# Gated mix of attention with a memory and a gated feed-forward layer: matmuls of ones and whole loads at the start, transposes in halves, rows split at the head of a step

## The chip, the cores and the metric

One NeuronCore of a Trainium2 chip runs the whole program. The metric is the device time of one execution in microseconds (us), the median of several runs. The five engines of the core run side by side and are told apart as in the profile: PE (matmul, with PEld for its weight loads), DVE (vector), ACT (scalar), POOL (general) and SP, whose queue issues nearly all DMAs.

## The reference

The input x has 2048 rows of 576 numbers. Two branches are computed from it and mixed row by row:

```python
x = A_x
g = _sigmoid((x * gate_w).sum(-1, keepdims=True))
a = _A_ref(x, A_wq, A_wk, A_wv, A_wo, A_beta)   # attention with a memory
b = _B_ref(x, B_w_gate, B_w_up, B_w_down)       # (gelu(x@w_gate) * (x@w_up)) @ w_down
return g * a + (1 - g) * b
```

Branch A has 32 heads of 18 numbers and cuts the 2048 rows into 4 segments of 512. In each segment it computes causal softmax attention within the segment, and beside it a read of a memory M that the earlier segments have written (`phi(q) @ M` over `phi(q) @ z`); the two are mixed by a gate for each head, and the result is multiplied by wo. Branch B has a hidden layer of 4608. All in float32.

## The kernel before, in words

To keep float32 accuracy on f16 matmuls, each operand is scaled by a power of two and split into a high and a low f16 word; a product is three matmuls (high by high, high by low, low by high). High words are made by ACT (a copy with a scale), low words by DVE or POOL (a subtraction). The scales come from sums of squares over the whole weight, so each weight is first summed (`square_sum`, `sum_squares`, L80), then scaled.

**The start** (L596 to L669). SP loads x of segment 0 in three pieces (`load_x16`, L123) and the values' weights wv in pieces of rows and of column halves (`load_v`, L415: half `b`, group `g` of `VG`), one half-piece behind each piece of x, then the weights of q and k (`load_qk`). While the scales aren't known, the values of segment 0 are computed in float32 from the raw x and wv (`first_words`, L512): four row blocks for the first column half in four PSUM banks, then four for the second half (banks `vb`). `scale_x` (L136), `scale_v` (L433) and `scale_sum(0, ...)` (L97, for q and k) each add up their sums with a matmul of ones (L85, or L140) and end in six to seven short DVE instructions. `low_x` (L157) makes the low words of x, `put_rows` (L480) takes the value rows out of PSUM, its second part `rest` being queued in `later` and run by `finish_later`. `make_qk` makes the two words of one tile of q and k weights (L103 on ACT, L104 on DVE), which `project` (L453) then multiplies with x.

**The segments** (L772 to L821). For segment s the value rows are `vrows(s, q, b)` (L505, banks `dn`, of which there are two, L312 to L315), with `key_rows`, `recall` and `memorize` for the memory between them (bank `U` and `pv`); then nine projections.

**The main loop** (`step`, L1078). 72 steps, each with one hidden tile f of 128 (two steps a tile) for a pair of segments c and e, and one pair of attention problems (2k and 2k + 1). Products of a pair of segments share matmuls in Strassen's manner (`product`, `rest`, L1012 to L1024) in the banks V, G (X) and U (Y). For each attention problem a: `score_piece` (L871) computes the scores on PE and takes their maximum on DVE (L887); `powers` (L892) is the exponential on ACT (L897, L900); `pair_rows(a, 0)` and `(a, 1)` (L902) make high words on ACT (L909) and low words on POOL (L910); `turn_rows` (L911) transposes both words by one DMA of 20 blocks of 128 by 128 (L915); `values` (L917) multiplies them with the values on PE (L929); `normalize` takes the result out on DVE. The hidden rows: `gelu` on ACT, `hidden` (L997) on DVE, `hidden_pair` (L999) splits them into words on ACT (L1001) and POOL (L1002), for c within the step, for e by way of `late_hidden` in the next one. They are in tiles `gl`, of which there are two. `weights_first`, `weights_high`, `weights_low` prepare weights for later steps: POOL's scaling is `scale_g` (L250) and `scale_d` (L287). `down` (L967, L975) is the last product of branch B and runs in pieces between the others.

The order on PE, ACT, DVE and POOL is the order in the program (a manual schedule of these four); SP's queue isn't written out by hand: a scheduler places each DMA, and each waits for its buffers and for the DMA eight before it.

**The end** (`finish`, L1200). In steps 67 to 71 the rows of wo are loaded, summed, scaled (`pair_of`, L102, over pieces of rows in the last three of these steps), then come the output products.

Of the kernel before, what the change touches and what calls it, by code (L numbers as in the profile page):

```python
# [10 lines left out]
F16 = mybir.dt.float16  # L11
# [7 lines left out]
P = 128  # L19
# [22 lines left out]
def kernel(ctx: ExitStack, tc: tile.TileContext, xs, wqk, wv, wo, wgu, wd, beta, out):  # L42
# [80 lines left out]
    def load_x16(c, then=None):  # L123
        x_raw[c] = []
        x_sq[c] = flat(wts.tile([P, 2, 16 * P], F16, name="pairg", tag="pairg", bufs=2)).bitcast(BF16)
        for i, (k0, n) in enumerate(XG):
            r = raw_tile()
            sp.dma_start(r[:, : n * L], flat(xs[c, :, k0 : k0 + n]))
            x_raw[c].append(r)
            if then:  # L130
                then(i)
# [264 lines left out]
    with tc.tile_pool(name="prj", bufs=2, side="right", reuse_waits="tile") as pp:  # L396
# [18 lines left out]
        def load_v(b, g):  # L415
            ks = slice(VG[g][0], VG[g][-1] + 1)
            sp.dma_start(raw_v[:, ks, VB[b]], wv[:, ks, VB[b]])

        def square_sum(o, r, on_act):
            if on_act:  # L420
                junk = pa.tile([P, D], F32, name="krow", bufs=2).bitcast(BF16)
                act.activation(junk[:, : r.shape[1]], r, AF.Square, accum_out=o)
            else:
                sum_squares(o, r)

        def stat_v(b):
            for k in range(KT):
                square_sum(wst[:, KT * b + k : KT * b + k + 1], raw_v[:, k, VB[b]], b == 1)

        def stat_qk(j):  # L430
            square_sum(wst[:, 10 + j : 11 + j], raw_qk[:, j], j % 2 or j == 8)

        def scale_v():  # L433
            scale_sum(1, wst[:, 0 : 2 * KT])

            dve.tensor_scalar(usc, wsc[:, 1:2], xsc[:, 0:1], 2.0**-14, OP.mult, OP.mult)
# [159 lines left out]
        with tc.manual_schedule(engines=ORDERED):  # L596
            pool.memset(ones, 1.0)
            pool.memset(onesb, 1.0)
            load_x16(0, lambda g: load_v(0, g))
            for g in range(3):  # L600
                load_v(1, g)
# [5 lines left out]
            stat_v(0)  # L607
# [4 lines left out]
            stat_v(1)  # L612
# [55 lines left out]
            dve.tensor_scalar(gh[:, 1], gh[:, 0], -1.0, 1.0, OP.mult, OP.add)  # L668
            outscale(0, 1)  # L669
# [161 lines left out]
    with tc.tile_pool(name="keep", bufs=2, side="right", reuse_waits="tile") as kp, ExitStack() as tail:  # L831
# [70 lines left out]
        def pair_rows(a, i):  # L902

            p = prob[a]
            if i == 0:
                pairs16[a] = ap_.tile([P, 2, 10 * P], F16, name="ph", bufs=2)
            h = pairs16[a]
            cols = (slice(6 * P, 10 * P), slice(0, 6 * P))[i]
            act.activation(h[:, 0, cols], p[:, cols], AF.Copy)  # L909
            pool.tensor_tensor(h[:, 1, cols], p[:, cols], h[:, 0, cols], OP.subtract)  # L910

        def turn_rows(a):
            prob.pop(a)
            turned_p[a] = ap_.tile([P, 20, P], F16, name="pt", bufs=2)
            sp.dma_start(turned_p[a], pairs16.pop(a).rearrange("p a b -> p (a b)"), transpose=True)  # L915
# [162 lines left out]
        def step(v):  # L1078
# [12 lines left out]
            done = (k - 5) // 4 if i4 == 3 and 0 <= (k - 5) // 4 < H // 2 else None  # L1091
            weights_first(fb, i4)
# [5 lines left out]
            if late_hidden:  # L1098
                hidden_pair(*late_hidden.pop())
# [13 lines left out]
            V = ahead.pop(v) if v in ahead else first_product(v)  # L1113
# [28 lines left out]
            if v == 0:  # L1142
                scales_out(1)
                scale_g(2)
# [55 lines left out]
        def finish(i):  # L1200
# [87 lines left out]
```

## Time and profile before

| | us |
|---|---|
| median of 3 runs | 1651.63 (1650.98 to 1653.91) |
| the profiled execution | 1651.15 |
| its span in the profile | 1649.4 |
| PE busy | 1624.4 |
| DVE, POOL, ACT busy | 1268.4, 1162.2, 1085.9 |
| DMA transposes of probabilities | 128 issues, median 3.13 each |

The span runs from the first to the last instruction; 1.75 us of the profiled execution lie around it. In the rows of the timeline the first two numbers are the start and the duration in us, then the engine, the line of the kernel, the operation, the tile written and those read, and in square brackets how long the engine had been idle before it and what ended that.

### The profile page before, as it was taken

What the parts mean: (1) busy time and instruction counts of PE and PEld (TensorE: products, weight loads), DVE (VectorE), ACT (ScalarE), POOL (GpSimd) and SP (SyncE); (2) the same over time, 40 slices, a digit from 0 to 9 for tenths busy, and PEclk for the clock granted to TensorE, in tenths of its full rate; (3) what the DMA queues carried; (4) which work ended last, traced back from release to release, by engine and by line L of the source; (5) the groups of instructions that cost most, each with busy time, mean ns of one, the idle gap of its engine ahead of it and who ended that gap; (6) DMA issues with size and microseconds to landing.
All of it is one profiled execution on the core that took longest, in us unless ns stands there. A gap on an engine that the chain in (4) does not pass through costs nothing.

```text
span 1649.4 us, 31958 instructions
## 1 busy us (share of the span) xinstructions
PE 1624.4 (98%) x11884; PEld 982.7 (60%) x11884; DVE 1268.4 (77%) x3138; ACT 1085.9 (66%) x1786; POOL 1162.2 (70%) x1057
## 2 busy tenths in 40 slices
PE   8999998999999999999999999999999999999999
PEld 4656753655566555666555565555566555565577
DVE  5666785888788888878887878788788888776643
ACT  6665446777777777776777677777777777763200
POOL 2232657788888889787979788788879798885300
PEclk9999999999999999999999999999999999999999
DMA  6632443565656575666656575757566565635451
GB/s 213 215 112 88 147 136 68 119 133 106 131 110 128 112 128 113 129 114 129 133 109 126 108 142 103 139 103 130 119 140 123 120 130 103 133 72 122 87 124 64
DMA packets 462348, 200.54 MB, mean 122 GB/s; under 512 B 421232, under 2 KB 431728, under 8 KB 461680
## 3 DMA queue, kind: packets, MB, share of 16 engines
q1 hardware_dynamic: 462192, 198.50, 55.2%
q8 instruction: 93, 1.52, 0.4%
q14 instruction: 63, 0.52, 0.1%
HBM read 82.60 MB, written 27.26 MB: 67 GB/s over the span
## 4 chain that ended last, share of the span: by engine, by line
PE 82%; DVE 5%; DMA 5%; ACT 4%; POOL 2%; issue 2%; SPq 0%; DVEq 0%; ACTq 0%
PE dn L975 21%; PE U L1017 14%; PE V L1017 10%; PE G L1017 10%; DMA pt<-ph 4%; PE st L881 3%; PE pv L929 3%; PE V L1024 3%; PE st L312 3%; PE dn L312 2%; PE st L302 2%; PE U L1024 2%; PE G L1024 2%; PE G L302 1%; ACT pf L900 1%
## 5 line engine op out<-in xcount | busy, mean ns | idle before, releaser
L975 PE MATMUL dn<-paird,hh 128*128 128x288 f16 x3402 | 486.3, 286 | 0.0
L1017 PEld LDWEIGHTS <-pairg 128*128 128x128 f16 x3024 | 289.9, 98 | 276.4 <-issue 4.3
L910 POOL TENSOR_TENSOR ph<-pf,ph 128x512 f16<-128x512 f32 (+1 forms) x256 | 371.3, 1450 | 84.1 <-ACT ph L909 52.3
L975 PEld LDWEIGHTS <-hh 128*128 128x128 f16 x3456 | 336.7, 97 | 137.7
L983 DVE SCALAR_TENSOR_TENSOR acc<-dn,ev,acc 128x288 f32<-128x288 f32 x535 | 268.2, 512 | 69.8 <-PE dn L975 66.7
L900 ACT ACTIVATE pf<-pf,mb,esc 128x512 f32<-128x512 f32 (+3 forms) x512 | 293.0, 642 | 2.9
L1002 POOL TENSOR_TENSOR hh<-gl,hh 128x512 f16<-128x512 f32 x144 | 188.6, 1310 | 140.1 <-ACT hh L1001 140.1
L887 DVE CUSTOM_DVE_ANT_0 pf<-st,mask 128x512 f32<-128x512 f32 (+3 forms) x512 | 228.8, 483 | 73.9 <-PE st L881 73.8
L1017 PE MATMUL U<-xt,pairg 128*128 128x512 f16 x864 | 210.0, 379 | 0.6 <-DVE gl L1136 0.6
L1017 PE MATMUL G<-x,pairg 128*128 128x512 f16 x864 | 210.0, 379 | 0.0
L909 ACT ACTIVATE ph<-pf 128x512 f16<-128x512 f32 (+1 forms) x256 | 184.3, 720 | 0.0
L283 POOL TENSOR_TENSOR pairg<-raw,pairg 128x512 f16<-128x512 f32 (+2 forms) x144 | 168.5, 1190 | 8.3 <-ACT pairg L279 8.3
L1007 ACT ACTIVATE gl<-gl,sc 128x512 f32<-128x512 f32 x144 | 103.4, 719 | 82.8 <-DVE gl L1151 41.2
L897 ACT ACTIVATE mb<-mx,esc 128x4 f32<-128x4 f32 x128 | 37.2, 290 | 183.4 <-DVE mx L887 183.3
L1001 ACT ACTIVATE hh<-gl 128x512 f16<-128x512 f32 x144 | 89.6, 622 | 81.4 <-DVE gl L997 81.4
L250 POOL TENSOR_SCALAR raw<-raw,sc 128x640 f32<-128x640 f32 x72 | 137.0, 1915 | 0.0
L881 PE MATMUL st<-kt,qt 72*128 72x512 f16 (+3 forms) x512 | 111.7, 299 | 1.6 <-DVE mx L887 1.6
L1017 PE MATMUL V<-x,pairg 128*128 128x512 f16 x432 | 105.0, 379 | 2.2 <-DVE gl L1116 2.1
L1017 PE MATMUL U<-x,pairg 128*128 128x512 f16 x432 | 104.8, 378 | 0.3 <-DVE gl L1151 0.3
L1017 PE MATMUL V<-xt,pairg 128*128 128x512 f16 x432 | 105.0, 379 | 0.0
L1007 ACT ACT_TABLE_LOAD x66 | 84.7, 1283 | 24.6 <-DVE gl L1137 23.9
L1024 PEld LDWEIGHTS <-pairg 128*128 128x128 f16 x576 | 56.3, 98 | 68.1
(252 smaller groups left out, 2527.6 us busy)
## 6 DMA issues: line engine op xcount, KB each, us to landing
raw<-in_wgu_dram SPq DMA_DIRECT2D x36, 640.0 KB
rawd<-in_wd_dram SPq DMA_DIRECT2D x36, 288.0 KB
qk<-stage SPq DMA_DIRECT2D x36, 256.0 KB
qt<-qk SPq DMA_DIRECT2D x128, 72.0 KB
kt<-qk SPq DMA_DIRECT2D x128, 72.0 KB
vp<-vstage SPq DMA_DIRECT2D x16, 296.0 KB
vt<-vp SPq DMA_DIRECT2D x16, 296.0 KB
orow<-oa SPq DMA_DIRECT2D x16, 288.0 KB
```

The costliest lines, as they stand in the source:

```text
L283: pool.tensor_tensor(spot(f, *p, 1), raw_g[f][:, p[0] : p[1]], spot(f, *p, 0), OP.subtract)
L881: pe.matmul(o[:, off : off + n], q[:, e * L + qi * P : e * L + (qi + 1) * P], kt[:, e * L : e * L + n], start=True, stop=True)
L887: dve.tensor_tensor_reduce(prob[a][:, COL[qi] : COL[qi + 1]], o[:, off : off + n], mask[:, L - n :], 1.0, -3e38, OP.add, OP.max, mx[a][:, ...
L900: act.activation(r, r, AF.Exp, bias=b[:, qi : qi + 1], scale=esc[:, 0, c : c + 1])
L909: act.activation(h[:, 0, cols], p[:, cols], AF.Copy)
L910: pool.tensor_tensor(h[:, 1, cols], p[:, cols], h[:, 0, cols], OP.subtract)
L975: pe.matmul(o[:, :NH], hh[:, a, q * P : (q + 1) * P], w[:, b, n * NH : (n + 1) * NH], start=i == 0, stop=i == 5)
L983: dve.scalar_tensor_tensor(av, o[:, :NH], ev, av, OP.mult, OP.add)
L1002: pool.tensor_tensor(hh[:, 1], t, hh[:, 0], OP.subtract)
L1007: act.activation(t, o, AF.Gelu_apprx_tanh, scale=scl[f // 2][0][:, 2 + c : 3 + c])
L1017: pe.matmul(o, w[:, i, (a + k) * P : (a + k + 1) * P], x[:, b + k], start=start and k == 0 and i == 0 and b == h, stop=k == 1 and i == 1, ...
L1024: pe.matmul(o, w[:, i, a * P : (a + 1) * P], x[:, b], start=False, stop=i == 1, skip_group_check=True)
```

## The change

- At the start 40 matmuls of a tile of ones with itself (128 by 128) run on PE into bank G, whose content is not used. The weights wv are loaded as whole rows, in three pieces instead of six: the first behind the first piece of x, the others behind all of x. Their sums of squares are taken over whole rows, all five on DVE (five halves were on ACT), and there are five sums instead of ten.
- Sums of squares of q and k weights: tile 8 goes from ACT to DVE, and the order among them, the low words of x and the taking out of rows is another. In the second column half, row blocks run in two pairs, the sums over q and k behind the second piece of the second pair; the last rows are finished before `outscale(0, 1)`.
- `vrows(s, 1, 0)` goes to bank U.
- `turn_rows` issues two transposes of 10 blocks each, one of the high words and one of the low words, into one tile, which is now taken at `pair_rows(a, 0)`. In the order of SP's queue the first of the two waits for ACT and the second for POOL, where the one before waited for POOL.
- `hidden_pair` of `late_hidden` comes at the head of a step, ahead of `weights_first`, `normalize`, `powers` and `pair_rows`.
- Where the first product V was computed ahead (steps 1 to 3), the first two pieces of scores come behind the first product X and the copy to Y.
- In step 0 `scale_g(2)` comes behind the first `hidden_pair`.
- `finish` scales wo in pieces of 2, 2 and 1 instead of 1, 2 and 2.

The diff, cut to its core:

```diff
-        def load_v(b, g):
+        def load_v(g):
             ks = slice(VG[g][0], VG[g][-1] + 1)
-            sp.dma_start(raw_v[:, ks, VB[b]], wv[:, ks, VB[b]])
+            sp.dma_start(raw_v[:, ks], wv[:, ks])
...
-        def stat_v(b):
-            for k in range(KT):
-                square_sum(wst[:, KT * b + k : KT * b + k + 1], raw_v[:, k, VB[b]], b == 1)
+        def stat_v(k):
+            square_sum(wst[:, k : k + 1], raw_v[:, k], False)
         def stat_qk(j):
-            square_sum(wst[:, 10 + j : 11 + j], raw_qk[:, j], j % 2 or j == 8)
+            square_sum(wst[:, 10 + j : 11 + j], raw_qk[:, j], j % 2)
...
-            pv = bank("dn", 2)
+            pv = bank("U") if (q, b) == (1, 0) else bank("dn", 2)
...
-            load_x16(0, lambda g: load_v(0, g))
-            for g in range(3):
-                load_v(1, g)
+            start = bank("G")
+            for _ in range(40):
+                pe.matmul(start[:, :P], onesb, onesb, start=True, stop=True)
+            load_x16(0, (lambda: load_v(0),))
+            for g in (1, 2):
+                load_v(g)
...
-            for j in (0, 2):
+            for j in (0, 2, 1, 3):
                 stat_qk(j)
+            low_x(0, 0)
             vb = [bank("G"), bank("U"), bank("st", 2), bank("st", 2)]
             for q in range(4):
                 put_rows(0, q, 0, va[q], usc, 1.0)
-            low_x(0, 0)
+            stat_qk(4)
+            low_x(0, 1)
+            for j in (6, 5, 8, 7):
+                stat_qk(j)
             finish_later()
-            low_x(0, 1)
-            for j in (1, 4, 3, 6, 5, 7, 8):
-                stat_qk(j)
+            low_x(0, 2)
...
-            for q in range(4):
+            for qs in ((0, 1), (2, 3)):
                 for k in range(KT):
-                    first_words(vb, 1, k, (q,))
-                if q == 1:
-                    scale_sum(0, wst[:, 10:19])
-                    low_x(0, 2)
-                    make_qk(0)
-                    put_rows(0, 0, 1, vb[0], usc, 1.0)
-                    put_rows(0, 1, 1, vb[1], usc, 1.0)
-                    finish_later()
-                    make_qk(1)
-                    outscale(0, 0)
-                if q == 2:
-                    act.activation(gh[:, 1], gh[:, 0], AF.Exp, scale=-1.0)
-                if q >= 2:
-                    put_rows(0, q, 1, vb[q], usc, 1.0)
+                    first_words(vb, 1, k, qs)
+                    if qs[0] and k == 1:
+                        scale_sum(0, wst[:, 10:19])
+                        make_qk(0)
+                        put_rows(0, 0, 1, vb[0], usc, 1.0)
+                        put_rows(0, 1, 1, vb[1], usc, 1.0)
+                        finish_later()
+                        make_qk(1)
+                        outscale(0, 0)
+                        act.activation(gh[:, 1], gh[:, 0], AF.Exp, scale=-1.0)
+            for q in (2, 3):
+                put_rows(0, q, 1, vb[q], usc, 1.0)
...
+            finish_later()
             outscale(0, 1)
...
         def turn_rows(a):
             prob.pop(a)
-            turned_p[a] = ap_.tile([P, 20, P], F16, name="pt", bufs=2)
-            sp.dma_start(turned_p[a], pairs16.pop(a).rearrange("p a b -> p (a b)"), transpose=True)
+            t, h = turned_p[a], pairs16.pop(a)
+            for i in range(2):
+                sp.dma_start(t[:, 10 * i : 10 * i + 10], h[:, i], transpose=True)
...
+            if late_hidden:
+                hidden_pair(*late_hidden.pop())
             weights_first(fb, i4)
             if on(k - 2):
                 normalize(2 * (k - 2) + 1)
             if on(k - 1):
                 powers(2 * k - 1)
                 pair_rows(2 * k - 1, 0)
-            if late_hidden:
-                hidden_pair(*late_hidden.pop())
...
-            scored(2 * k, 0)
-            scored(2 * k, 1)
+            if not there:
+                scored(2 * k, 0)
+                scored(2 * k, 1)
             product(X, f, A11, x1, 0, 4, True)
             dve.tensor_copy(Y, X)
+            if there:
+                scored(2 * k, 0)
+                scored(2 * k, 1)
...
                 scales_out(1)
-                scale_g(2)
...
             hidden_pair(f, c, g0)
+            if v == 0:
+                scale_g(2)
...
-                for k in ((0,), (1, 2), (3, 4))[i - 2]:
+                for k in ((0, 1), (2, 3), (4,))[i - 2]:
                     pair_of(wos[k], rows[k], wsc[:, 2:3])
```

More of the change, by code (lines that the diff above doesn't have):

```diff
@@ L121, with load_x16 @@
     XG = ((0, 2), (2, 2), (4, 1))
-    def load_x16(c, then=None):
+    def load_x16(c, then=()):
         x_raw[c] = []
@@ L129, in load_x16 @@
             x_raw[c].append(r)
-            if then:
-                then(i)
+            if i < len(then):
+                then[i]()
     def square_x(c, k):
@@ L424, in square_sum @@
                 sum_squares(o, r)
-        def stat_v(b):
-            for k in range(KT):
-                square_sum(wst[:, KT * b + k : KT * b + k + 1], raw_v[:, k, VB[b]], b == 1)
+        def stat_v(k):
+            square_sum(wst[:, k : k + 1], raw_v[:, k], False)
         def stat_qk(j):
-            square_sum(wst[:, 10 + j : 11 + j], raw_qk[:, j], j % 2 or j == 8)
+            square_sum(wst[:, 10 + j : 11 + j], raw_qk[:, j], j % 2)
         def scale_v():
-            scale_sum(1, wst[:, 0 : 2 * KT])
+            scale_sum(1, wst[:, 0:KT])
             dve.tensor_scalar(usc, wsc[:, 1:2], xsc[:, 0:1], 2.0**-14, OP.mult, OP.mult)
@@ L606 @@
                 square_x(0, k)
-            stat_v(0)
+            for k in range(KT):
+                stat_v(k)
             turns.update(of=0)
@@ L611 @@
                 first_words(va, 0, k, range(4))
-            stat_v(1)
             scale_x(0)
@@ L906, in pair_rows @@
                 pairs16[a] = ap_.tile([P, 2, 10 * P], F16, name="ph", bufs=2)
+                turned_p[a] = ap_.tile([P, 20, P], F16, name="pt", bufs=2)
             h = pairs16[a]
@@ L1112, in step @@
             x1, x2_, t = x16[c], x16[e], xt[p]
-            V = ahead.pop(v) if v in ahead else first_product(v)
+            there = v in ahead
+            V = ahead.pop(v) if there else first_product(v)
             X, Y = bank("G"), bank("U")
```

## The prediction

> **What bounds the kernel now.** I read the page first: the span and the busy shares.
>
> ```profile
> span 1649.4 us, 31958 instructions
> PE 1624.4 (98%) x11884; PEld 982.7 (60%) x11884; DVE 1268.4 (77%) x3138; ACT 1085.9 (66%) x1786; POOL 1162.2 (70%) x1057
> ```
>
> TensorE (PE) is busy for 98% of the span; 1649.4 - 1624.4 = 25.0 us are left. The change takes no work from PE, so it can win only idle stretches of PE and matmuls that run slowly. So the view to read is that of the waits, for PE alone, the longest in total first.
>
> ```profile
> PE pv L929 <- DMA pt<-ph: 7.0, 9, 1.5
> PE dn L516 <- DMA acc<-in_wv_dram: 5.7, 2, 5.4
> PE V L1017 <- DVE gl L1116: 2.1, 2, 1.7
> PE st L881 <- DVE mx L887: 1.6, 3, 0.6
> PE st L315 <- DVE wo L104: 0.9, 1, 0.9
> PE dn L312 <- DVE vstage L498: 0.9, 1, 0.9
> PE U L1017 <- DVE gl L1136: 0.6, 1, 0.6
> ```
>
> The columns are total us, times, longest. Nearly every part of the change aims at one of these rows. A wait of PE that goes shortens the span by its length if nothing else is late within that time, because PE has work queued behind all of them.
>
> **The start.** The timeline of the first 36 us, PE, DVE, ACT and POOL, with one row of the view of windows (its last columns are the granted clock, DMA share and GB/s).
>
> ```profile
> 0.92 0.20 POOL L598 MEMSET onesb<- 128x128 bf16 x1
> 5.38 2.26 PE L516 MATMUL dn<-acc,raw 128*128 128x288 f32 x4 [5.38 <-DMA acc<-in_wv_dram]
> 9.93 1.41 PE L516 MATMUL dn<-acc,raw 128*128 128x288 f32 x4 [0.37 <-DMA acc<-in_wv_dram]
> 12.14 1.24 PE L140 MATMUL st<-pairg,onesb 128*128 128x512 bf16 x5
> 13.22 1.13 PE L516 MATMUL dn<-acc,raw 128*128 128x288 f32 x4
> 15.16 1.13 PE L516 MATMUL dn<-acc,raw 128*128 128x288 f32 x4
> 18.51 0.82 DVE L80 CUSTOM_DVE_ANT_0 junk<-acc 128x640 bf16<-128x640 f32 x1
> 26.45 0.17 DVE L99 TENSOR_REDUCE sv<-V 128x1 f32<-128x9 f32 x1 [0.54 <-PE V L85]
> 27.40 0.83 ACT L103 ACTIVATE wp<-acc,wsc 128x640 f16<-128x640 f32 x1 [2.26 <-DVE wsc L94]
> 27.46 0.75 DVE L163 SCALAR_TENSOR_TENSOR x<-raw,xsc,x 64x512 f16<-64x512 f32 x1
> 28.26 0.88 DVE L104 SCALAR_TENSOR_TENSOR wp<-acc,wsc,wp 128x640 f16<-128x640 f32 x1
> 31.91 2.76 PE L302 MATMUL G<-x,wp 128*128 128x512 f16 x12
> 33.57 0.89 DVE L104 SCALAR_TENSOR_TENSOR wp<-acc,wsc,wp 128x640 f16<-128x640 f32 x1 [1.63 <-ACT wp L103]
> 35.82 2.75 PE L302 MATMUL st<-x,wp 128*128 128x512 f16 x12 [0.71 <-DVE gate L500]
> 3.00:8.00 5.00, 2.62 (x6) 1.94 (x7) 0.57 (x2) 1.88 (x4) 4.59 (x14) 1.00 1.03 375
> ```
>
> The group of four matmuls from 13.22 takes 15.16 - 13.22 = 1.94 us; the first group, from 5.38, is still running when the wait before 9.93 begins (9.93 - 0.37 = 9.56), 4.18 us. So the first groups run at about half speed, though the granted clock reads 1.00. **Matmuls of ones:** 40 pairs can run from about 1.2 us, when the ones are written. Their price is not in the trace. The nearest row has five of 512 columns in 1.24 us, 0.25 each; a quarter of the columns is 0.06, doubled at the slow rate 0.12, so 2.4 to 5.0 us for 40, and 20 us at worst if each takes as long as one of 512 columns does slowly. I take 5.0, the slow rate: they end at 6.2. **Whole loads:** the first matmul now needs 0.592 MB of values' weights (128 x 1156 x 4 bytes) behind the same x, where it needed 0.295 MB: 0.297 MB more at 375 GB/s is 0.8 us, so 5.38 becomes 6.2. The ones hide in that wait; if the load costs nothing they cover it from 5.4 on, at 0.8. The second group no longer waits (0.37), since its rows came in the first load.
>
> The first groups took until about 9.93 + 2.2 = 12.14. Warm, two groups take 2 x 1.94 = 3.9 and end at 10.1, so PE and the chain of scales behind it run 2.0 us earlier. If the clock is slow until 8, half of that is lost.
>
> The Trainium skill's page TensorE: Matmul & The Clock Gate, Part 1, says the array starts at half rate and is released after about 3.4 us of sustained matmuls in a free-running window; the trace agrees with half rate (1.94 against 4.18), but took about 5 us (5.38 to between 9.93 and 11). By the page's figure the ones would have it released at about 5, by the row at about 6.2 to 7; the sum differs by less than 0.5 us.
>
> What is late next is DVE. It begins the statistics of q and k at 18.51, now 16.4 to 16.5, and reached the scale at 26.45 after a wait of 0.54. It now has one statistic more (0.82 and the reading of its sum, some 0.87) and the last 0.75 us of x (L163) ahead of the scale: 26.45 - 2.05 - 0.54 + 0.87 + 0.75 = 25.5. Then ACT's L103 is at 26.4, and L104 follows at once at 27.3 (no L163 between), so the first projection's weights are there at 28.2. PE gets there at 10.1 + 1.2 for the squares' sum + 32 matmuls x 0.485 + 0.5 for two small sums = 27.3, so it waits about 0.9: the first projection starts at 28.2 instead of 31.91. The second one waited until 35.82 for the gates of the last two rows, because DVE formed two more pieces of weights first (from 33.57, 0.9 each) and waited 1.63 for ACT ahead of them. Now the rows stand ahead of these: 35.82 - 1.63 - 1.8 - 0.9 (the start of L104, 28.26 against 27.3) = 31.5, or when PE is free, 28.2 + 2.9 = 31.1; ACT's copies may hold it to 32.7. Against 35.82 that is 3.1 to 4.3; I take **3.5** (0.9 if the clock stays slow, and a loss of 1 if the ones run to 11). Values' rows in bank U take away the wait at L312: bank U has been read by then, **0.85**.
>
> **Halves of probabilities.** The two views of single lines for the two kinds of DMA transposes, then the timeline of one pair, with POOL, ACT, SP and PE.
>
> ```profile
> L915 SPq DMA_TRANSPOSE pt<-ph x128: 2940/3130/5710, 275.3 to 1476.9; - x128
> L1198 SPq DMA_TRANSPOSE ot<-orow x16: 1277/1380/2302, 1507.6 to 1596.9; - x16
> 902.34 3.42 SPq L851 DMA_DIRECT2D kt<-qk  x1
> 906.31 10.39 SPq L915 DMA_TRANSPOSE pt<-ph  x2
> 1009.58 0.74 DVE L997 SCALAR_TENSOR_TENSOR gl<-U,sc,gl 128x512 f32<-128x512 f32 x1
> 1010.70 0.30 ACT L897 ACTIVATE mb<-mx,esc 128x4 f32<-128x4 f32 x1 [2.77 <-DVE mx L887]
> 1015.60 0.83 ACT L909 ACTIVATE ph<-pf 128x768 f16<-128x768 f32 x1
> 1018.29 1.74 POOL L1002 TENSOR_TENSOR hh<-gl,hh 128x512 f16<-128x512 f32 x1
> 1019.99 1.64 POOL L910 TENSOR_TENSOR ph<-pf,ph 128x768 f16<-128x768 f32 x1
> 1021.65 3.02 SPq L915 DMA_TRANSPOSE pt<-ph  x1
> 1028.25 0.68 PE L929 MATMUL pv<-vt,pt 128*128 128x37 f16 x20 [0.81 <-DMA pt<-ph]
> ```
>
> SP issues the transpose as POOL ends the low words (1019.99 + 1.64 = 1021.63, issue at 1021.65) and needs 3.13 us (median) for 20 blocks. The other transposes have 9 blocks and need 1.38: (3.13 - 1.38) / 11 = 0.16 a block and nothing fixed. So a half of 10 blocks costs about 1.55. The high half waits for ACT alone (1016.4) and is out before POOL ends, so the low half lands 3.13 - 1.55 = 1.6 us earlier than the whole does. No wait is longer than 1.5, so those released by POOL go. The one behind 906.31 was held by SP's queue (kt's issue from 902.34 for 3.42 us), and both halves still stand behind that; I leave it 1.0 and the others 0.3: 7.0 - 1.3 = **5.7**. Bounds: 0, if a half costs what a whole does, and 7.0. The instruction's own fixed part I cannot see apart from issue.
>
> [...]
>
> **Last rows split at the head.** ACT's copy and POOL's subtraction of a pair's last hidden rows move ahead of POOL's scaling, DVE's normalizing and ACT's powers. ACT was idle 2.77 us before 1010.70 and the rows were ready at 1009.58 + 0.74 = 1010.3, so the copy (0.6) delays the powers by 0.3 and later saves 0.6. On POOL the same 1.7 us moves from behind its first low words to ahead of its scaling: it ends the low words no later unless it has to wait for ACT first, by up to 1 us. Queued behind it are weights of a later step. Net 0, bounds -0.5 to +1 us of landing, inside the 1.6 won.
>
> **First scaling behind rows, and scores behind the first product.** The ramp, POOL, PE and DVE in the timeline:
>
> ```profile
> 245.47 3.74 POOL L250 TENSOR_SCALAR raw<-raw,sc 128x640 f32<-128x640 f32 x2
> 249.18 1.15 POOL L1002 TENSOR_TENSOR hh<-gl,hh 128x512 f16<-128x512 f32 x1
> 251.11 1.46 PE L1017 MATMUL V<-x,pairg 128*128 128x512 f16 x6 [1.68 <-DVE gl L1116]
> 281.59 0.69 DVE L1136 COPY gl<-U 128x512 f32<-128x512 f32 x1 [2.52 <-POOL hh L1002]
> ```
>
> POOL's scaling of 3.74 us stands ahead of the rows (L1002) that free the buffer for L1116. Behind them, the rows end 3.7 us sooner: the wait of 1.68 goes. L1136 at 281.59 waited for the last rows of the step before, which now stand at the head: its 0.6 on PE goes. Of L881's 1.6, two waits lie where X's product now runs first, but the copy behind them hangs on DVE, which is busy without a break, so I count nothing (bound 1.0). Together 1.7 + 0.6 less 0.2: **2.1**.
>
> **The tail.**
>
> ```profile
> 1569.09 2.44 DVE L104 SCALAR_TENSOR_TENSOR wo<-wor,wsc,wo 128x576 f16<-128x576 f32 x2
> ```
>
> One of these two pieces (1.2 us) is now done a step earlier; L315's wait of 0.9 goes: **0.85**.
>
> **The sum.** The profiled execution took 1651.15 us (span 1649.4 and 1.75 around it), the median is 1651.63, so nothing is to be shifted. 3.5 + 0.85 + 5.7 + 2.1 + 0.85 = 13.0: 1651.15 - 13.0 = **1638.2 us**.
>
> **Rivals.**
> - *A half lands no sooner.* The completion may be bound by something besides issue: PE waited at 1028.25 though issue ended at 1024.67. For it: 3.6 us between these two. Against it: 9 and 20 blocks scale. The 5.7 falls to 1.3: 1642.6.
> - *The ones do not warm the array, or run past the loads.* The start gives 0.9 instead of 3.5: 1640.8; with the ones until 11, 1642.7. Against it: the row of 1.24 us for five.
> - *SP's queue becomes the bound (slower).* If a half has a fixed price such that two cost over 3.13 + the 5 us that the high half is ahead, the low half lands later than now, in every one of 64 pairs. 1.5 us late costs at least 13.5 on the 9 waits that exist: 1651.15 - 7.3 + 13.5 = 1657. It decides from a half of about 4 us. Against it: 1.38 for 9 blocks.
> - *It does not do what it says:* new waits of DVE take up what is won, 1649 to 1653.
>
> **Numbers.** Forecast 0.64, no sooner 0.13, ones 0.11, SP 0.07, nothing 0.05. The first three give faster by over 0.2% (3.3 us, about what a measurement of this kernel can tell from no change): 0.88; within 0.2%: 0.05; slower: 0.07. All wins at their upper bounds (4.3, 0.85, 7.0, 2.3 + 1.0, 0.9) are 16.4: 1634.8, taken as 1635. The two middle rivals together (0.9 and 1.3) are 1645.2. The range is 1635 to 1645.
>
> **What would show it.** Forty matmuls ahead of the first data and groups of 1.94 us from the first on; the first projection at about 28 and the second at about 32; issues of about 1.55 us, with almost no wait of PE for pt; no PE wait for L1116 of 1.7 at about 246, none at L312 and L315. It is wrong if the issues of halves last as long as those of wholes, if the first groups still take 4 us, or if PE's idle time shows new rows of DVE.

## The result, and the profile after

The changed kernel takes 1661.74 us (median of 6 runs, 1661.26 to 1664.11), the kernel before took 1652.12 beside it (1650.98 to 1653.91): the ratio is 1.0059, with a 95% interval of 1.0046 to 1.0072. It is slower by 9.6 us; the forecast was 1638.2 and its range ended at 1645. The page of the profiled execution:

```profile
span 1660.4 us, 32241 instructions
PE 1630.5 (98%) x11924; PEld 988.0 (60%) x11924; DVE 1270.0 (76%) x3140; ACT 1088.6 (66%) x1774; POOL 1151.0 (69%) x1057
```

The span is 11.0 us longer. The waits of PE in the changed kernel (total us, times, longest):

```profile
PE V L1023 <- DVE gl L1123: 21.3, 26, 1.4
PE pv L935 <- DMA pt<-ph: 1.3, 2, 1.0
```

L1023, L1123 and L935 are the lines that were L1017, L1116 and L929. Every wait that the change aimed at has shrunk: pt from 7.0 to 1.3, the load of wv from 5.7 to 0.2, and those at L312 and L315 are gone. In their place stands one row: PE waits 21.3 us, where it waited 2.1, for DVE's copy of the first product V into `gl`, the g1 copy.

The place of the loss is read from when one instruction of each step runs. The first g1 copy starts at 237.6 us before and 233.2 after: the start has won 4.4. The product V of step 3 on PE (L1017, now L1023) begins at 276.60 before and 270.71 after: 5.9 won so far. The g1 copy of the last step starts at 1554.7 before and 1566.9 after: 12.2 late. So steps 3 to 71 lost 18.1 us, and the tail behind won 1.2 (94.7 to the end of the span before, 93.5 after).

In the loop, 19.3 of the waits of V and -5.7 of pt give 13.6. The other 4.5 us stand in no row of waits; where such time lies is worked out below from a pair of runs.

The steps of the start, in the timeline of the changed kernel (start, duration, idle time before it in brackets):

```profile
1.19 4.45 PE L601 MATMUL G<-onesb 128*128 128x128 bf16 x40 [1.19 <-POOL onesb L597]
5.84 1.56 PE L515 MATMUL dn<-acc,raw 128*128 128x288 f32 x4 [0.21 <-DMA acc<-in_wv_dram]
8.21 1.13 PE L515 MATMUL dn<-acc,raw 128*128 128x288 f32 x4
...
28.82 2.75 PE L302 MATMUL G<-x,wp 128*128 128x512 f16 x12 [0.52 <-DVE gate L499]
31.84 2.75 PE L302 MATMUL st<-x,wp 128*128 128x512 f16 x12
```

The ones end at 5.64, the first group of row blocks takes 8.21 - 5.84 = 2.37 us (4.18 before); the two projections start at 28.82 and 31.84, where 28.2 and about 32 were forecast (31.91 and 35.82 before). The transposes:

```profile
L921 SPq DMA_TRANSPOSE pt<-ph x256: 1252/1357/5496, 267.3 to 1488.3; - x128
```

A half takes 1.36 us (median), where 1.55 was forecast. So the parts do, one by one, what they were to do, and something else costs more than all of them win.

### The profile page after: what moved, and what is told of

It reads as the page before. It is cut to its first block, busy times and chain, and to the rows that moved or that the text cites. A ratio compares the mean times of both kernels' runs of the same rounds, so it can differ in the third digit from the quotient of the medians.

```text
span 1660.4 us, 32241 instructions
## 1 busy us (share of the span) xinstructions
PE 1630.5 (98%) x11924; PEld 988.0 (60%) x11924; DVE 1270.0 (76%) x3140; ACT 1088.6 (66%) x1774; POOL 1151.0 (69%) x1057
## 3 DMA queue, kind: packets, MB, share of 16 engines
q1 hardware_dynamic: 465344, 198.52, 61.2%
## 4 chain that ended last, share of the span: by engine, by line
PE 83%; DVE 12%; issue 2%; DMA 1%; ACT 1%; POOL 0%; SPq 0%; DVEq 0%; POOLq 0%; ACTq 0%
PE dn L981 21%; PE U L1023 17%; PE V L1023 10%; PE G L1023 9%; PE pv L935 3%; PE st L885 3%; PE V L1030 3%; PE st L312 3%; DVE pf L891 2%; PE U L1030 2%; PE G L1030 2%; PE dn L312 2%; PE st L302 2%; DVE junk L80 2%; DVE acc L989 2%
## 5 line engine op out<-in xcount | busy, mean ns | idle before, releaser
L1023 PEld LDWEIGHTS <-pairg 128*128 128x128 f16 x3024 | 289.9, 98 | 303.0 <-issue 29.0
L915 POOL TENSOR_TENSOR ph<-pf,ph 128x512 f16<-128x512 f32 (+1 forms) x256 | 365.9, 1440 | 59.0 <-ACT ph L914 59.0
L989 DVE SCALAR_TENSOR_TENSOR acc<-dn,ev,acc 128x288 f32<-128x288 f32 x535 | 269.2, 513 | 100.7 <-PE dn L981 97.7
L1008 POOL TENSOR_TENSOR hh<-gl,hh 128x512 f16<-128x512 f32 x144 | 171.5, 1191 | 191.7 <-ACT hh L1007 191.7
L891 DVE CUSTOM_DVE_ANT_0 pf<-st,mask 128x512 f32<-128x512 f32 (+3 forms) x512 | 229.0, 484 | 60.0 <-PE st L885 59.7
L1023 PE MATMUL G<-x,pairg 128*128 128x512 f16 x864 | 210.0, 379 | 0.0
L1023 PE MATMUL U<-xt,pairg 128*128 128x512 f16 x864 | 209.8, 379 | 0.0
L283 POOL TENSOR_TENSOR pairg<-raw,pairg 128x512 f16<-128x512 f32 (+2 forms) x144 | 175.0, 1236 | 8.2 <-ACT pairg L279 8.2
L914 ACT ACTIVATE ph<-pf 128x512 f16<-128x512 f32 (+1 forms) x256 | 178.4, 720 | 0.0
L250 POOL TENSOR_SCALAR raw<-raw,sc 128x640 f32<-128x640 f32 x72 | 139.3, 1946 | 0.0
L1023 PE MATMUL V<-x,pairg 128*128 128x512 f16 x432 | 104.9, 378 | 21.3 <-DVE gl L1123 21.3
L1023 PE MATMUL U<-x,pairg 128*128 128x512 f16 x432 | 104.8, 378 | 0.3 <-DVE gl L1161 0.3
L1023 PE MATMUL V<-xt,pairg 128*128 128x512 f16 x432 | 105.0, 379 | 0.0
L1161 DVE TENSOR_TENSOR gl<-U,gl 128x512 f32<-128x512 f32 x72 | 49.8, 692 | 58.2 <-PE U L1023 58.2
L279 ACT ACTIVATE pairg<-raw 128x512 f16<-128x512 f32 (+2 forms) x144 | 82.8, 616 | 17.4 <-POOL raw L250 9.4
```

The source lines that it names most:

```text
L250: pool.tensor_scalar(r, r, scl[f // 2][0][:, 0:1], None, OP.mult)
L283: pool.tensor_tensor(spot(f, *p, 1), raw_g[f][:, p[0] : p[1]], spot(f, *p, 0), OP.subtract)
L891: dve.tensor_tensor_reduce(prob[a][:, COL[qi] : COL[qi + 1]], o[:, off : off + n], mask[:, L - n :], 1.0, -3e38, OP.add, OP.max, mx[a][:, ...
L989: dve.scalar_tensor_tensor(av, o[:, :NH], ev, av, OP.mult, OP.add)
L1008: pool.tensor_tensor(hh[:, 1], t, hh[:, 0], OP.subtract)
L1023: pe.matmul(o, w[:, i, (a + k) * P : (a + k + 1) * P], x[:, b + k], start=start and k == 0 and i == 0 and b == h, stop=k == 1 and i == 1, ...
```

## The new wait, read in one step

This is the stretch ahead of such a wait in the changed kernel, with DVE, POOL, ACT and PE:

```profile
380.40 0.63 ACT L1007 ACTIVATE hh<-gl 128x512 f16<-128x512 f32 x1 [2.49 <-DVE gl L1003]
380.62 0.94 DVE L989 SCALAR_TENSOR_TENSOR acc<-dn,ev,acc 128x288 f32<-128x288 f32 x2
381.11 1.15 POOL L1008 TENSOR_TENSOR hh<-gl,hh 128x512 f16<-128x512 f32 x1 [1.09 <-ACT hh L1007]
381.48 1.40 DVE L80 CUSTOM_DVE_ANT_0 junk<-rawd 128x576 bf16<-128x576 f32 x1
382.22 1.25 POOL L270 TENSOR_TENSOR raw<-raw 128x256 f32<-128x256 f32 x1
383.41 0.97 DVE L949 SCALAR_TENSOR_TENSOR osum<-osum,gha,ord 128x72 f32<-128x72 f32 x2
384.36 0.73 POOL L272 TENSOR_TENSOR raw<-raw 128x256 f32<-128x256 f32 x1
384.41 0.84 DVE L953 TENSOR_TENSOR ob<-ob,osum 128x144 f32<-128x144 f32 x1
385.18 0.68 DVE L1123 COPY gl<-V 128x512 f32<-128x512 f32 x1
385.91 0.59 PE L1023 MATMUL V<-x,pairg 128*128 128x512 f16 x2 [0.93 <-DVE gl L1123]
```

And the same step where the hidden rows are back in their old place (the first experiment below, all else as changed):

```profile
378.95 0.94 DVE L989 SCALAR_TENSOR_TENSOR acc<-dn,ev,acc 128x288 f32<-128x288 f32 x2
379.81 0.75 DVE L80 CUSTOM_DVE_ANT_0 junk<-rawd 128x576 bf16<-128x576 f32 x1
379.92 1.22 POOL L272 TENSOR_TENSOR raw<-raw 128x256 f32<-128x256 f32 x1
381.09 0.97 DVE L949 SCALAR_TENSOR_TENSOR osum<-osum,gha,ord 128x72 f32<-128x72 f32 x2
381.22 0.75 POOL L273 TENSOR_TENSOR raw<-raw 128x256 f32<-128x256 f32 x1
382.09 0.31 DVE L953 TENSOR_TENSOR ob<-ob,osum 128x144 f32<-128x144 f32 x1
382.32 0.68 DVE L1123 COPY gl<-V 128x512 f32<-128x512 f32 x1
383.14 1.46 PE L1023 MATMUL V<-x,pairg 128*128 128x512 f16 x6
```

From the first of the two L989 to the g1 copy DVE needs 385.18 - 380.62 = 4.56 us in the one and 382.32 - 378.95 = 3.37 in the other, with the same instructions and no idle time between. Two of them are longer. L80 takes 1.40 instead of 0.75: it starts while POOL's subtraction L1008 runs (381.11 + 1.15 = 382.26) and ends 0.62 behind its end. L953 takes 0.84 instead of 0.31, beside L272 (384.36 + 0.73 = 385.09, and L953 ends at 385.25). Where DVE is first, POOL pays: L272 takes 1.22 behind an L80 that started 0.11 ahead of it. DVE's instructions that take their main input out of PSUM keep their time whatever POOL runs beside them: over the whole changed kernel each L989 takes 0.50 to 0.52 and each L1123 0.68 to 0.69. So the two engines take turns at something.

The Trainium skill's page SBUF — State Buffer, Who interferes with whom, names it: VectorE and GpSimd share one pair of ports under an exclusive lock, and a VectorE instruction with two inputs in SBUF contends with a GpSimd instruction that reads SBUF. Its section SBUF: two separate sides has the instruction that starts first keep the pair for its whole length. These rows agree: L949, L953 and L80 (which takes one tile as both of its inputs) have two inputs in SBUF, L989 and L1123 have not, and the later one ends 0.2 to 0.6 us behind the other. Rows beside POOL's scaling L250, which has one tensor as input, agree only in part:

```profile
825.82 1.16 POOL L1008 TENSOR_TENSOR hh<-gl,hh 128x512 f16<-128x512 f32 x1 [1.10 <-ACT hh L1007]
826.13 1.46 DVE L965 SCALAR_TENSOR_TENSOR oh<-ob,wsc,oh 128x576 f16<-128x576 f32 x1
826.95 4.25 POOL L250 TENSOR_SCALAR raw<-raw,sc 128x640 f32<-128x640 f32 x2
828.10 0.50 DVE L949 SCALAR_TENSOR_TENSOR osum<-osum,gha,ord 128x72 f32<-128x72 f32 x2
828.63 0.31 DVE L953 TENSOR_TENSOR ob<-ob,osum 128x144 f32<-128x144 f32 x1
```

```profile
362.96 1.16 POOL L1008 TENSOR_TENSOR hh<-gl,hh 128x512 f16<-128x512 f32 x1
363.12 1.86 DVE L949 SCALAR_TENSOR_TENSOR osum<-osum,gha,ord 128x72 f32<-128x72 f32 x2
364.10 3.75 POOL L250 TENSOR_SCALAR raw<-raw,sc 128x640 f32<-128x640 f32 x2
365.98 1.24 PE L1023 MATMUL V<-x,pairg 128*128 128x512 f16 x5 [0.68 <-DVE gl L1123]
```

In the first of these steps L965 waits out L1008 (1.46 instead of 0.81). L250 is 1.15 us old when the two L949 begin, and these keep their short time, 0.50 together, as L953 does. In the second the first L949 waits out L1008, the second begins 0.04 behind the start of L250 and takes 0.84, and the two need 1.86 together. That holds throughout the changed kernel: of the 41 L949 that begin beside an L250, 23 begin within 0.04 us of its start, take 0.84 and end 0.88 behind that start, and 18 begin over 1.1 us behind it and take 0.28 to 0.29. So L250 holds DVE only early in its 1.9 us or more, where by the page it would for its whole length; these rows decide, and why it is so was not found.

So two steps in a round of four are late, for two reasons. In the second, which has the sums (L270 to L273), PE waits 0.93, from step 5 to step 65; in the first, which has the scaling L250, it waits 0.68, from step 8 to step 28.

The groups show it over the run, in the kernel before and then in the changed one (count, busy us, mean ns):

```profile
L943 DVE SCALAR_TENSOR_TENSOR osum<-osum,gha,ord 128x72 f32<-128x72 f32 x128 | 52.1, 447 | 2.3
L947 DVE TENSOR_TENSOR ob<-ob,osum 128x144 f32<-128x144 f32 x64 | 27.1, 424 | 2.2
L959 DVE SCALAR_TENSOR_TENSOR oh<-ob,wsc,oh 128x576 f16<-128x576 f32 x16 | 12.9, 809 | 0.0
```

```profile
L949 DVE SCALAR_TENSOR_TENSOR osum<-osum,gha,ord 128x72 f32<-128x72 f32 x128 | 75.8, 633 | 2.3
L953 DVE TENSOR_TENSOR ob<-ob,osum 128x144 f32<-128x144 f32 x64 | 36.8, 576 | 2.2
L965 DVE SCALAR_TENSOR_TENSOR oh<-ob,wsc,oh 128x576 f16<-128x576 f32 x16 | 18.8, 1176 | 0.0
```

These three normalize the results of a pair and stand right ahead of the g1 copy. They take 131.4 us after and 92.1 before. DVE's sum hardly moves (1268.4 and 1270.0), because other groups got shorter in return, L80's form of 640 numbers above all (93.9 to 66.9 us).

So **theory 1**: POOL's subtraction of the hidden rows at the head of the step has to wait for ACT (1.09 us above), takes its turn beside L80, and pushes POOL's sums or scaling of weights onto DVE's chain ahead of the g1 copy. **Theory 2**, the rival: once PE no longer waits for pt, it comes earlier and any DVE would be late. **Theory 3**: the halved transposes (DMA busy 61.2% of the span instead of 55.2%) slow the others.

## The experiments

Ratios are to the kernel before on the same chip, whose median was 1655.0 to 1657.1 there; 0.001 is 1.66 us. Differences in us below are worked out from the ratios, unless medians are named. The waits are those of one profiled execution.

| kernel | time us | ratio, 95% interval | pt waits | waits of V |
|---|---|---|---|---|
| e14: changed | 1663.14 | 1.0049 (1.0037 to 1.0062) | 1.4 | 21.3 |
| e1: changed, hidden rows back | 1639.66 | 0.9894 (0.9877 to 0.9910) | 3.2 | 2.0 |
| e12: the same again | 1638.61 | 0.9893 (0.9879 to 0.9907) | 0.8 | 2.0 |
| e2: before + hidden rows at the head | 1672.34 | 1.0093 (1.0078 to 1.0109) | 3.0 | 19.7 |
| e3: changed, whole transposes | 1665.60 | 1.0056 (1.0039 to 1.0073) | 5.1 | 18.7 |
| e4: before + halves | 1649.61 | 0.9950 (0.9934 to 0.9967) | 3.2 | 2.1 |
| e5: changed, only POOL back | 1640.52 | 0.9903 (0.9886 to 0.9919) | 2.9 | 2.0 |
| e6: changed, weights ahead | 1652.39 | 0.9974 (0.9963 to 0.9986) | 3.9 | 10.1 |
| e7: changed, normalize behind | 1668.14 | 1.0069 (1.0054 to 1.0084) | 1.4 | 2.0 |
| e8: changed, no sums | 1649.69 (one run) | - | 1.5 | 6.4 |
| e11: e12 with whole transposes | 1652.18 | 0.9978 (0.9967 to 0.9989) | 12.9 | 2.0 |
| e10: e12 without ones | 1639.81 | 0.9903 (0.9889 to 0.9916) | 2.5 | 2.0 |
| e9: before + start | 1656.20 | 1.0002 (0.9993 to 1.0011) | 13.3 | 2.1 |
| e13: before + start + bank U | 1651.52 | 0.9978 (0.9969 to 0.9986) | 9.6 | 2.1 |
| e15: e12 without bank U | 1641.62 | 0.9915 (0.9901 to 0.9928) | 3.2 | 2.0 |
| e16: before | 1653.04 (one run) | - | 7.4 | 2.1 |

**The hidden rows back, and alone.** e1 is the changed kernel with this; e2 is the kernel before with the opposite move:

```diff
-            if late_hidden:
-                hidden_pair(*late_hidden.pop())
             weights_first(fb, i4)
...
                 pair_rows(2 * k - 1, 0)
+            if late_hidden:
+                hidden_pair(*late_hidden.pop())
```

> The changed kernel, only late_hidden's hidden_pair back in its old place (behind normalize, powers and the first pair_rows). Theory 1 (the move itself: POOL's scaling and sums of weights start about 1.2 us later in a step, lie beside DVE's instructions ahead of the g1 copy and lengthen these, so that PE waits 0.93 and 0.68 us for the copy once in four steps, 19 us in all): the waits of V for the g1 copy fall from 21 us to 2 or 3, and the time from 1661.7 to 1638 to 1643. Theory 2 (the waits for pt that went were covering DVE; PE now comes earlier and any DVE would be late): waits for the g1 copy stay above 12 us, time 1655 or more. Theory 3 (the halves of transposes load the DMA engines and slow others): no change, 1660 to 1663.

> The kernel before, with the head placement of late_hidden's hidden_pair alone. Theory 1: slower by the new waits and the stretched work, 16 to 23 us, 1668 to 1674, with V waiting for the g1 copy once or twice in four steps. Theory 2: PE still has its pt waits (or DVE's lateness swallows them), 1650 to 1654. Theory 3: 1650 to 1653, since no transpose is split.

e1 takes 1639.66, 17.5 us less than before, and the waits of V fall to 2.0. e2, which has nothing else of the change, is 15.4 us slower than before and has the waits:

```profile
PE V L1017 <- DVE gl L1116: 19.7, 24, 1.7
...
PE pv L929 <- DMA pt<-ph: 3.0, 4, 1.6
```

This move turned the sign. Theory 2 is out as a cause: in e2 the transposes are whole, and the waits of V come all the same; in e1 they are halved, and no such wait comes. Part of it stays: in e2 the pt waits fall from 7.0 to 3.0 with no better transpose, since PE now comes later.

The rest of the loss is found by placing the matmuls of the changed kernel beside those of e12 (e1 once more, in the table) one by one, since both run the same ones in the same order. Ahead of V, 19.3 us more are waits. Another 5.0 us lie ahead of V in 32 steps and 3.0 ahead of the next product, U, in 46 steps, and both count as busy time of PE (1630.5 against 1622.8). There, too, PE is held by DVE: U begins 0.05 us behind the end of DVE's copy of X to Y (L1128) in those 46 steps. So a late DVE costs more than the rows of waits show. PE's busy time by itself is no measure of this: it is 1625.6 in e1, with the same kernel as e12.

**Whole transposes, and halves alone.** The diff of e3 (e4 is its opposite on the kernel before, e11 the same on e12):

```diff
+            turned_p[a] = ap_.tile([P, 20, P], F16, name="pt", bufs=2)
+            sp.dma_start(turned_p[a], pairs16.pop(a).rearrange("p a b -> p (a b)"), transpose=True)
-            for i in range(2):
-                sp.dma_start(t[:, 10 * i : 10 * i + 10], h[:, i], transpose=True)
```

> The changed kernel with one transpose of 20 blocks for each problem again. Theory 1: the waits for the g1 copy stay; the pt waits come back in part, since PE is held by DVE first: 1661 to 1667. Theory 2: the pt waits come back and the g1 waits shrink by as much: 1660 to 1663. Theory 3: without the second issue the time falls to 1640 to 1652.

> The kernel before with the two transposes of 10 blocks alone. Theory 1: the pt waits fall from 7.0 to about 1.3 with nothing new in their place: 1645 to 1648. Theory 2: what pt no longer takes appears as waits for the g1 copy: 1651 to 1656. Theory 3: 1655 to 1665.

> The kernel of e1_hidden_back with one whole transpose for each problem. What the halves are worth where DVE isn't in the way. By the forecast's term (5.7 us): 5 to 7 us slower than e12 and pt waits of 7 to 9 us instead of 3. If halves are worth nothing: within 2 us of e12.

Theory 3 is out: without the second issue (e3) the time doesn't fall, and halves alone win. What they win depends on who is late: 8.3 us on the kernel before (5.5 to 10.9 by the interval), 13.6 between the medians of e11 and e12 (the runs of e11 spread over 7 us, and its profiled one lies 2.4 above the median), and nothing in the changed kernel (1.0056 in e3, 1.0049 and 1.0059 for the change): there the waits are 5.1 + 18.7 = 23.8 with whole transposes and 1.3 + 21.3 = 22.6 with halves. A PE that is held by DVE has no use for an earlier transpose.

**Which engine's part of the move.** In e5 ACT's copy stays at the head and POOL's subtraction goes back:

```diff
+            low = hidden_pair(*late_hidden.pop()) if late_hidden else None
             weights_first(fb, i4)
...
                 pair_rows(2 * k - 1, 0)
+            if low:
+                low()
```

In e6 `hidden_pair` stands behind `weights_first` and ahead of `normalize`, so that only POOL's two pieces change places.

> The changed kernel with ACT's copy of the last hidden rows at the head of the step and POOL's subtraction back behind the first low words. Theory 1a (POOL's subtraction is the harm: DVE's instructions with two operands in SBUF and POOL's run one after the other, and the subtraction pushes the sums of weights onto DVE's chain ahead of the g1 copy): no waits for the g1 copy in the loop (2 to 3 us in all), 1637 to 1642 on the scale of before at 1651.6, ratio 0.989 to 0.993. Theory 1b (ACT's copy ahead of the powers is the harm): waits of V above 12 us, ratio 1.002 to 1.007.

> The changed kernel with hidden_pair at the head but behind weights_first: only POOL's two pieces change places, sums or scaling of weights first, then the subtraction. Theory 1a: the sums lie where they lay before, so the waits of V for the g1 copy fall to 2 to 4 us, ratio 0.989 to 0.993; what is left of a difference to the old place is the subtraction ahead of the first low words. Theory 1b: waits above 12 us, ratio 1.002 to 1.007.

e5 is as fast as e1 (0.9903 and 0.9894, intervals overlap): ACT's copy ahead of the powers costs nothing that shows. It is POOL's subtraction. e6 was expected to be as fast, and isn't: it loses 13 us to e1, with 10.1 us of waits of V. The sums lie where they lay, but now the subtraction itself meets the chain, at its last link:

```profile
382.00 0.75 POOL L273 TENSOR_TENSOR raw<-raw 128x256 f32<-128x256 f32 x1
382.72 1.15 POOL L1008 TENSOR_TENSOR hh<-gl,hh 128x512 f16<-128x512 f32 x1
382.88 1.16 DVE L953 TENSOR_TENSOR ob<-ob,osum 128x144 f32<-128x144 f32 x1
383.96 0.68 DVE L1123 COPY gl<-V 128x512 f32<-128x512 f32 x1
384.69 1.46 PE L1023 MATMUL V<-x,pairg 128*128 128x512 f16 x6 [0.60 <-DVE gl L1123]
```

L953, 0.31 alone, takes 1.16: it starts 0.16 behind L1008 and ends 382.88 + 1.16 - 382.72 - 1.15 = 0.17 behind it. So theory 1 holds in its core, the turns, but "the sums are pushed" was too narrow: whichever of POOL's sums or subtractions lies there does it. In the old place the subtraction runs beside DVE's work out of PSUM (in e1 from 384.74 to 385.91, beside L1128, L989 and L891).

**The g1 copy out of the chain.** e7 puts `normalize` (and the copy of results that reads it) behind the g1 copy.

```diff
-            if on(k - 2):
-                normalize(2 * (k - 2) + 1)
...
             dve.tensor_copy(g1, V)
+            if on(k - 2):
+                normalize(2 * (k - 2) + 1)
```

> The changed kernel, hidden_pair at the head, but DVE's normalize (five instructions, 1.9 to 3.1 us) and the copy of results that reads it behind the g1 copy. If the time is lost only because the g1 copy is late behind the lengthened instructions, the waits of V go (2 to 3 us left in all) and the time falls to a ratio of 0.989 to 0.994. If the lengthened instructions cost the same wherever they stand, because DVE as a whole is late, other waits of PE for DVE (st for mx, U for gl) take the place: ratio above 1.0.

The second outcome came, at another place than named:

```profile
PE U L1023 <- DVE U L1128: 22.1, 39, 1.0
PE V L1023 <- DVE gl L1119: 2.0, 3, 1.4
```

The g1 copy is in time, and the next copy, of X to Y in bank U, is late 39 times. At the head of a step DVE has several things that PE needs soon, and the chain of normalizing delays whichever stands behind it.

**Without the sums.** e8 takes POOL's sums and differences of weights out of the loop, so that the products use weights that weren't summed:

```diff
-            if i4 == 1 and fb:
-                sums_g(n0 + 1)
             if i4 == 2 and fb:
...
-                sums_g(n0 + 2)
```

> The changed kernel without the sums and differences of gate and up weights on POOL in the loop (sums_g left out in two of four steps, so the products use unsummed weights). Theory 1a: in the step behind it L949 and L953 lose the 0.47 and 0.53 us that they wait for POOL, and L80 keeps its 0.6: the wait of V of 0.93 in that step goes or falls under 0.1, the one of 0.68 in the step with the scaling stays until half of the run; waits of V 5 to 9 us instead of 21, time 1643 to 1649. If POOL's work beside it has no part in the lengthening, both waits stay, 1658 to 1662.

```profile
PE V L1023 <- DVE gl L1120: 6.4, 10, 1.4
...
L953 DVE TENSOR_TENSOR ob<-ob,osum 128x144 f32<-128x144 f32 x64 | 19.7, 308 | 2.2
```

As theory 1 has it: 6.4 us of waits instead of 21.3, and L953 at 0.31 in the mean. The waits of 0.93 are gone and the six of 0.68, in the steps with the scaling, stay. On DVE and PE not one instruction was changed. The time was 1649.69 in a single run, beside 1657.14 for before: just above the 1643 to 1649 that were expected, and 9 us above e5. So the sums are the larger part of the loss and not the whole; DVE's copy of X to Y still holds U in 46 steps here.

**The start.** e9 is the kernel before with the whole start of the change, e13 adds bank U, e10 takes the 40 matmuls of ones from e12, and e15 puts this back in e12:

```diff
-            pv = bank("U") if (q, b) == (1, 0) else bank("dn", 2)
+            pv = bank("dn", 2)
```

> The kernel before with the whole change of the start alone (ones, whole loads, order of statistics and rows), not bank U. By the forecast 3.5 us faster than before (0.9 to 4.3), ratio 0.9975 to 0.9985, the first projection at 28 to 29 instead of 31.9, the first g1 copy at 233 to 234 instead of 237.3.

> The kernel of e1_hidden_back without the 40 matmuls of ones. If they warm the array as the forecast has it, without them the first groups of four run 4 us instead of 1.9 and all the start behind them is 1.5 to 3 us later: 1.5 to 3 us slower than e12. If the wait for the second column half and DVE's sums set the start (the first projection waits for DVE anyway), 0 to 0.7 us slower.

> The kernel before with the change of the start and with bank U for the second row block's values. If the start's gain was given back at L312 (3.0 us of waiting in e9, released by DVE L497 behind an ACT that had waited 3.4 us for a DMA of stage), bank U uncovers it: 3 to 4.5 us faster than before, ratio 0.9973 to 0.9985, the first g1 copy near 233. If the start is worth nothing at all on this chip: ratio 0.999 to 1.001.

> The kernel of e12 (hidden_pair in its old place) with vrows back in the banks dn. If bank U is what lets the start's gain through, its price is that of L312 in e9, 2.5 to 3.5 us more than e12's ratio of 0.9893: 0.9908 to 0.9915, with a wait at L312 of about 3. By the forecast's term it is 0.85: 0.9896 to 0.9901.

e9 was expected to win 3.5 us and wins nothing. Its projection does start earlier, at 28.94. Most of that is given back 35 us on, in the timeline of e9:

```profile
60.94 0.60 ACT L462 ACTIVATE stage<-G 128x512 f16<-128x512 f32 x1 [3.43 <-DMA qk<-stage]
62.68 0.41 ACT L492 ACTIVATE vstage<-dn 128x288 f16<-128x288 f32 x1
63.50 0.46 DVE L497 SCALAR_TENSOR_TENSOR vstage<-dn,vstage 128x288 f16<-128x288 f32 x1
64.01 2.31 PE L312 MATMUL dn<-wv,x 128*128 128x288 f16 x11 [3.01 <-DVE vstage L497]
```

PE reaches the first values' rows of segment 1 (L312) at 57.21, where it was 61.07 before: 3.9 us earlier. But ACT waits for a store of q and k to free `stage`, and that has it going at 60.94 instead of 62.04, only 1.1 earlier. Behind ACT the first block's rows stay in the bank that PE needs at L312, so the third chain there starts at 64.01 (65.72 before), and the fourth at 68.08 against 68.22. The first g1 copy then starts at 237.5, as before (237.6), and in e13 at 232.7. With bank U (e13) PE has another bank, and the start wins 3.6 us (2.3 to 5.1). e15 points the same way from the other side, though its interval overlaps that of e12: without bank U there are 2.1 us of waiting at L312 and the ratio is 0.0022 (3.6 us) higher. The ones are worth 0.0010 of the ratio, 1.7 us, which the intervals don't tell from nothing; in the trace of e10, which lacks them, the first group takes 3.97 us instead of 2.37 and the first g1 copy starts at 235.2 instead of 232.7.

**The machine's part.** e14 and e16 are the two kernels once more.

> The kernel of e1_hidden_back once more, beside the next three on one chip, to have their differences from it: ratio 0.988 to 0.992.

> The changed kernel itself, to stand beside e16 (the kernel before) and the experiments on one chip. Ratio 1.004 to 1.007; pt waits 1 to 3 us, waits of V for the g1 copy 19 to 22 us.

> The kernel before itself, for its trace on this chip: the median of before was 1652.1 in the first runs and is 1655.5 to 1657 here. If whole transposes land later here, the pt waits are 10 to 14 us instead of the 7.0 of the trace that the forecast was made from, and with them the halves' larger worth is explained. If the pt waits are 7 as there, something else in the halves is worth the rest.

e16 has 7.4 us of pt waits in its one execution, so nothing speaks for later landing on that chip as the reason why halves won more than forecast. But e9, e13 and e11, with whole transposes and a changed start, have 13.3, 9.6 and 12.9, and the two profiles of one kernel with halves 3.2 and 0.8. Part of this may be which execution was profiled: that of e9 took 1663.82, the longest of eleven with a median of 1656.20. Whether and why whole transposes land too late oftener once the start has moved wasn't settled.

## Why the prediction was wrong, step by step

- **What bounds the kernel.** Right that PE sets the time and that its waits are what can be won. What wasn't read is how much room other work has before it becomes a wait: the g1 copy in the kernel before has next to none. In such a step of it the copy starts at 995.03 and takes 0.68, and PE starts on V at 995.86: 0.15 us behind the end, with no wait. Where V is held by the copy, as at 385.91, it starts 0.05 behind the end, so 0.1 us of room is left.
- **Last rows split at the head: the step that failed.** The forecast had "Net 0, bounds -0.5 to +1 us of landing", and of POOL "Queued behind it are weights of a later step". It is 15.4 us on the kernel before (e2) and about 1.6% with the rest of the change (1.0049 against 0.9893, 26 us), by way of PE's waits for the g1 copy. The queue of POOL was looked at for what those weights delay by being late; what they meet was not. In the trace of before, DVE's row L80 has a mean of 1361 ns for the form of 640 numbers, where single ones take 0.81 us, and single L947 take 0.31 to 0.85: the turns between the two engines were there to see.
- **The wait that POOL adds for ACT** was seen ("unless it has to wait for ACT first, by up to 1 us") and measures 1.09 in the step shown. Its follow-up was not.
- **The start and bank U**, 3.5 + 0.85 = 4.35: together 3.6 (e13, 2.3 to 5.1). The split between them was wrong: the start is worth nothing that shows alone (e9) and bank U uncovers it. They are one term.
- **Halves**, 5.7: the mechanism right (a half 1.36 us, pt waits 0.8 to 3.2), the size not one number: 8.3 on the kernel before (e4, whose 5.5 to 10.9 just holds the 5.7), 13.6 with the rest of the change (e12 against e11), and 0 behind a late DVE. The forecast took one profile's 7.0 us of waits as the whole stock.
- **The ramp**, 2.1: from 4.4 to 5.9 won by step 3, 1.5. The wait of 1.68 fell to 0.21, and a new one of 1.42 stands at 270.71. **The tail**, 0.85: 1.2 by position. Neither was run by itself.
- **The sum without the failed step**: 13.0 was forecast, e12 has 0.9893 (17.7 us, 15.4 to 20.0 by the interval) with it undone. The halves, worth more there than forecast, would account for the surplus; no run splits it up.
- **The rivals.** "New waits of DVE take up what is won" had the right mechanism at 0.05 and a wrong ceiling: it was priced at what is won, though waits in one or two steps of every four for 1200 us have no such bound. The forecast's own sign of being wrong, new rows of DVE in PE's idle time, is what came. The halves, at a median of 1.36 us, are far from the 4 us of the rival of SP's queue, and the ones did speed up the first group (2.37, and 3.97 without them).

The best kernel of the study is the change with the hidden rows in the old place: 1638.61 us, 0.9893 of before.

## What to carry to other kernels

When a piece moves on one engine, look at what it comes to lie beside on the other engines, not only at what is queued behind it: two engines can block each other with no semaphore between them, and then a group's mean hides a short and a long form. Count, for each thing that the bounding engine waits for, how late it may become before it is a wait; where that is near 0.1 us, a move "off the path" is on it. And a gain at one place counts only if nothing fixed in time stands between it and the end: the start's 3 us were lost to a store 35 us later until another bank let PE past.

## What the runs showed of the hardware that was not expected

- DVE's instructions with two inputs in SBUF and POOL's sums and subtractions took turns: 0.31 became 0.84 and 1.16 (L953), 0.75 became 1.40 (L80), each ending 0.2 to 0.6 us behind POOL's. POOL's scaling (L250) held an L949 that began within 0.04 us of its start (0.84) and let one through that began over 1.1 us behind it (0.29). DVE's reads of PSUM kept their time (L989 at 0.5).
- DVE's lateness cost PE 8 us beyond the rows of waits (5.0 ahead of V, 3.0 ahead of U), in time that counts as busy.
- The same kernel had 3.2 and 0.8 us of pt waits in two profiled executions.
